# Row maximum of the widest score tile: two parts chained, in place of two parts joined

## The chip, the cores and the metric

The kernel runs on one core of a Trainium2 chip. The metric is the device time of one execution in microseconds (us). Five engines work side by side, each through its own queue of instructions in a fixed order: TensorE (PE, matrix products and transposes into PSUM), VectorE (DVE), ScalarE (ACT), GpSimd (POOL) and SyncE (SP, which here only issues DMAs; ACT issues some too). They meet through semaphores.

## The reference

Causal attention with a decay bias for 4 batches of 8 heads, 576 positions, head size 64, then two feed-forward layers over all 2304 tokens:

```python
scores = scale * np.matmul(q, k.transpose(0, 1, 3, 2))
cum = np.cumsum(np.maximum(s, 0.0), axis=-1)
bias = -(cum[:, :, :, None] - cum[:, :, None, :])
scores = np.where(causal, -1000000000.0, scores + np.minimum(bias, 0.0))
scores = scores - np.max(scores, axis=-1, keepdims=True)
attn = np.exp(scores)
attn = attn / (np.sum(attn, axis=-1, keepdims=True) + 1e-09)
out = np.matmul(attn, v)
...
h = x @ w_in;  e = np.exp(h - h_max);  solu = h * e / (sum(e) + 1e-09)
x = (layer norm of solu, times g_ln) @ w_out
h = x @ w2_in;  out = (h * np.clip(h + 3.0, 0.0, 6.0) / 6.0) @ w2_out
```

The change concerns the row maximum (`np.max`) that is subtracted before `exp`.

## The kernel before, in words

**The scores of a head.** The 576 queries of a head are cut into five tiles of 128, 128, 128, 96 and 96 rows (`SZ`, L197). Because of the causal mask, tile t only needs the keys up to its own end, so its width w is 128, 256, 384, 480 or 576. PE writes the scores into a PSUM bank of 512 columns. The fifth tile, 576 wide, doesn't fit into one bank: `pieces_of` (L518) cuts it into two pieces of 288 columns in two banks, and the other four tiles are one piece each. There are 32 heads, so 32 such wide tiles with 64 pieces.

**The row maximum.** `tops` (L497) runs on DVE once per piece: it adds the mask (0 or -1e30) to the negative scores, writes them to SBUF (`ys`) and collects the smallest value of each row, which is the negative row maximum, into a column of `nmax`. On the chip this is a pair: the pass itself (CUSTOM_DVE_ANT_0) and a short one that reads the accumulator out (DVE_READ_ACCUMULATOR2_ANT). The first piece's minimum goes to column t (here 4), the second's to the spare column NQ (5). `both` in `exps` (L507, its instruction on L508) then takes the smaller of the two columns, and `exp` (L510) runs on ACT over the whole 576 columns with column t as its bias.

**Where the results go.** `norm` (L580) takes the reciprocal of the row sums on DVE and scales the rows on POOL (L587). `tr` transposes them on PE (L614), ACT and DVE copy them to SBUF (L618), `av` multiplies with V on PE (L642). Heads 0 to 7 (batch 0) are done in pairs by `qk_whole` (products on L544), heads 8 to 31 one at a time by `qk` (products on L571). For these, `prep_qk` (L433) loads q and k of a pair (`load_qk`, DMA on L381), transposes them on PE (L450), splits them into a high and a low part on ACT (L458) and DVE (L462), and copies these by DMA into two operand stacks, `stack0` for the even and `stack1` for the odd head (L468, L469, gates L472). A stack is overwritten only when the products of the head that used it are done. The DMAs of q and k of pair p+1 are held until the copies of the keys of pair p into `stack1` have begun (`begun`, L371).

**The first feed-forward layer** runs among the attention of batches 1 to 3: products on L713, statistics (L724 to L754), transposes on L779, products on L800. Its weights arrive as 64-bit words and are decoded by `split64` (L286) on ACT, DVE and POOL during batch 0 and the start of batch 1; their DMAs (raw_wi, raw_wo) are issued by ACT, 512 KB each. The second layer (L957, L988) follows, from about 390 us on.

**The order.** Nothing is issued in the order of the source. Each `plan.add` (L53) records an operation with its engine, an assumed cost, and the keys that it reads and writes. `Plan.emit` (L88) then simulates the engines with these assumed costs, always takes the ready operation with the lowest record number, gives out the eight PSUM banks as they come free, and emits the operations of all engines in the order of the simulated starts. So an operation that is taken out, or a dependency that is added, can move every later operation on every engine. The joining operation is one of these records, at an assumed 0.2 us:

```python
if len(pieces) > 1:
    plan.add("DVE", 0.2, both, reads=[f"nmax{h}_{NQ}"], writes=[f"nmax{h}_{t}"])
```

Of the kernel before, what the change touches and what calls it, by code (L numbers as in the profile page):

```python
# [16 lines left out]
ALU = mybir.AluOpType  # L17
# [144 lines left out]
def dve(n):  # L162
    return 0.15 + 0.00104 * n
# [6 lines left out]
def act(n, extra=0.17):  # L170
    return extra + 0.00085 * n
# [6 lines left out]
def pe(n):  # L178
    return max(0.107, 0.000447 * n)
# [3 lines left out]
def kernel(ctx, tc, q, k, v, s, w_in, w_out, g_ln, w2_in, w2_out, out):  # L183
    nc = tc.nc
# [14 lines left out]
    NQ = len(SZ)  # L199
# [11 lines left out]
    nmax = const.tile([P, NH, NQ + 1], F32, name="nmax")  # L211
# [20 lines left out]
    at = ExitStack()  # L232
# [5 lines left out]
    def bank(key):  # L238
        return banks[plan.bank[key]]


    mask = ap1.tile([P, 480 + P], F32, name="mask")
# [107 lines left out]
    plan = Plan()  # L350
# [17 lines left out]
    raws, vs, ys, x_b, pts, hls = {}, {}, {}, {}, {}, {}  # L368
# [31 lines left out]
    def gates_at(p, j):  # L400
        return stack_t[p % 2][j * D : (j + 1) * D, 2:4, :]
# [91 lines left out]
    def y_key(h, t):  # L493
        p = h // 2
        return f"yz{p}/{h}_{t}" if p < NPAIR and p % 2 else f"y{h}_{t}"

    def tops(h, t, c0, c1, at, key):  # L497

        n, w = SZ[t], ST[t] + SZ[t]
        nc.vector.tensor_tensor_reduce(  # L500
            out=ys[h, t][:n, c0:c1], in0=bank(key)[:n, : c1 - c0], in1=mask[:n, 480 + n - w + c0 : 480 + n - w + c1], scale=-1.0, scalar=3.0e38,
            op0=ALU.add, op1=ALU.min, accum_out=nmax[:n, h, at : at + 1])

    def exps(h, t, pieces):
        n, w = SZ[t], ST[t] + SZ[t]

        def both():  # L507
            nc.vector.tensor_tensor(nmax[:n, h, t : t + 1], nmax[:n, h, t : t + 1], nmax[:n, h, NQ : NQ + 1], ALU.min)  # L508

        def exp():  # L510
            y = ys[h, t]
            nc.scalar.activation(out=y[:n], in_=y[:n], func=AF.Exp, bias=nmax[:n, h, t : t + 1], scale=-1.0, accum_out=sums[:n, h, t : t + 1])  # L512

        if len(pieces) > 1:
            plan.add("DVE", 0.2, both, reads=[f"nmax{h}_{NQ}"], writes=[f"nmax{h}_{t}"])
        plan.add("ACT", act(w, 0.46), exp, reads=[f"nmax{h}_{t}"] + [f"{y_key(h, t)}/{c0}" for c0, _, _ in pieces], writes=[f"{y_key(h, t)}/e", f"sums{h}_{t}"])

    def pieces_of(t):  # L518
        w = ST[t] + SZ[t]
        return [(0, w, t)] if w <= 512 else [(0, w // 2, t), (w // 2, w, NQ)]  # L520

    def qk_whole(p, t):

        n, w = SZ[t], ST[t] + SZ[t]
        heads = (2 * p, 2 * p + 1)
        z_key = f"yz{p}" if p % 2 else None

        def mm(c0, c1, keys):
            if z_key and not (heads[0], 0) in ys:
                for h, tag in zip(heads, ("zh", "zl")):  # L530
                    z = bcp.tile([P, KFF, 2 * P], F32R, tag=tag, name=f"{tag}y{p}", bufs=1).rearrange("p a n -> p (a n)").bitcast(F32)
                    o = 0
                    for i in range(NQ):
                        ys[h, i] = z[:, o : o + ST[i] + SZ[i]]
                        o += ST[i] + SZ[i]
            elif c0 == 0 and not z_key:
                for h in heads:
                    ys[h, t] = ap2.tile([P, w], F32, tag=f"y{t}", name=f"y{h}_{t}")
            for m in range(2):
                for j in range(2):  # L540
                    r = slice(j * D, (j + 1) * D)
                    g, hl = gates_at(p, j), hls[f"HL{p}"].bitcast(F32)[r]
                    a, b = (hl[:, 0, :], hl[:, 1, :]) if m else (g[:, 0, :], g[:, 1, :])
                    nc.tensor.matmul(bank(keys[j])[:n, : c1 - c0], lhsT=a[:, ST[t] : w], rhs=b[:, c0:c1], start=(m == 0), stop=(m == 1))  # L544

        pieces = pieces_of(t)
        for c0, c1, at in pieces:
            keys = [f"sc{h}_{t}_{c0}" for h in heads]
            new = []
            if z_key and z_key not in plan.born:  # L550
                new = [("z", 1, z_key)]
            elif c0 == 0 and not z_key:
                new = [(f"y{t}", 2, f"y{h}_{t}") for h in heads]
            plan.add("PE", 5 * pe(c1 - c0) + 0.1, lambda c0=c0, c1=c1, keys=keys: mm(c0, c1, keys),
                     reads=[f"HL{p}/{x}{c}" for x in "qk" for c in (0, 3)] + [f"G{p}", f"whole{p % 2}"], writes=keys, new=new, bank=keys, after=[f"sc{heads[0]}_{t}_0"] if c0 else [])
            for h, key in zip(heads, keys):
                plan.add("DVE", dve(c1 - c0), lambda h=h, c0=c0, c1=c1, at=at, key=key: tops(h, t, c0, c1, at, key), reads=[key],
                         writes=[f"{y_key(h, t)}/{c0}", f"nmax{h}_{at}"])
        for h in heads:
            exps(h, t, pieces)  # L560

    def qk(h, t):
        n, w = SZ[t], ST[t] + SZ[t]
        pieces = pieces_of(t)

        def mm(c0, c1, key):
            if c0 == 0:
                ys[h, t] = ap2.tile([P, w], F32, tag=f"y{t}", name=y_key(h, t))
            ss = stack_t[h % 2]
            for m in range(2):  # L570
                nc.tensor.matmul(bank(key)[:n, : c1 - c0], lhsT=ss[:, 2 - 2 * m, ST[t] : w], rhs=ss[:, 3 - 2 * m, c0:c1], start=(m == 0), stop=(m == 1))  # L571

        for c0, c1, at in pieces:
            key = f"sc{h}_{t}_{c0}"
            plan.add("PE", 2 * pe(c1 - c0), lambda c0=c0, c1=c1, key=key: mm(c0, c1, key),
                     reads=[f"S{h // 2}_{h % 2}/{x}" for x in "qkg"], writes=[key], new=[(f"y{t}", 2, y_key(h, t))] if c0 == 0 else [], bank=key)
            plan.add("DVE", dve(c1 - c0), lambda c0=c0, c1=c1, at=at, key=key: tops(h, t, c0, c1, at, key), reads=[key], writes=[f"{y_key(h, t)}/{c0}", f"nmax{h}_{at}"])
        exps(h, t, pieces)

    def norm(h):  # L580
# [291 lines left out]
    for b, share in enumerate(SHARES):  # L872
# [10 lines left out]
        while cost < share or in_sum:  # L883
# [3 lines left out]
            c, f, _, in_sum = side.pop(pick)  # L887
# [118 lines left out]
    plan = Plan()  # L1006
# [11 lines left out]
    plan = Plan()  # L1018
# [68 lines left out]
```

## Time and profile before

| | us |
|---|---|
| median of 3 runs | 865.81 (861.31 to 867.98) |
| the profiled execution, its time | 866.15 |
| its span, first to last instruction | 864.3 |
| PE busy in the span | 817.4 (95%) |
| DVE busy | 485.1 (56%) |
| ACT busy | 401.3 (46%) |
| POOL busy | 225.8 (26%) |

The mean granted TensorE clock of the span is 0.986 of full speed. Busy time of PE is the sum over matmul records that overlap a little, so start-to-start distances are the safer measure of its pace. "Idle before" is the time an engine stood still just before an instruction, with the instruction that released it.

### The profile page before, as it was taken

Reading aid. Unit: us, or ns where it says so; the run is one execution under the profiler, and the core shown is the slowest. Engines: PE = TensorE matmul, PEld = TensorE weight load, DVE = VectorE, ACT = ScalarE, POOL = GpSimd, SP = SyncE. Lnnn points to the kernel's source line nnn. Section 1 sums busy time; section 2 is a strip of 40 time slices with the busy share of each in tenths; the row PEclk is TensorE's granted clock in tenths of the full one; section 3 lists DMA queues with packets and bytes.
Section 4 is the critical chain, followed back from the end, with each engine's and each line's share of the span. In section 5 each row is a group of like instructions: output and inputs, shape, how many; then the busy total and the mean of one; then the engine's idle time right before and its main releaser. Section 6 shows DMA issues by size and latency. Waiting matters only on the chain.

```text
span 864.3 us, 13509 instructions
## 1 busy us (share of the span) xinstructions
PE 817.4 (95%) x4816; PEld 690.2 (80%) x4816; DVE 485.1 (56%) x1205; ACT 401.3 (46%) x928; POOL 225.8 (26%) x323
## 2 busy tenths in 40 slices
PE   4987869999999999998989999999999999999998
PEld 3666648888888878886989899998888888888886
DVE  5897897556856576637673999943322232213221
ACT  2875566555755566635353555443221322232222
POOL 2676664524632355234330211200000000000000
PEclk9998979999999999999999999999999999999999
DMA  7468762646645455314313444213000200010001
GB/s 185 122 165 180 165 156 67 144 109 132 126 99 131 114 126 121 86 30 151 103 65 116 147 146 127 94 49 98 0 1 2 76 22 1 1 49 1 1 1 49
DMA packets 93667, 76.85 MB, mean 89 GB/s; under 512 B 62080, under 2 KB 75904, under 8 KB 93600
## 3 DMA queue, kind: packets, MB, share of 16 engines
q1 hardware_dynamic: 91296, 67.60, 31.5%
q10 hardware_dynamic: 2304, 8.39, 3.1%
q8 instruction: 38, 0.62, 0.3%
q14 instruction: 29, 0.24, 0.1%
HBM read 44.71 MB, written 10.03 MB: 63 GB/s over the span
## 4 chain that ended last, share of the span: by engine, by line
PE 78%; DMA 9%; DVE 6%; POOL 3%; SPq 2%; ACT 1%; issue 1%; ACTq 0%; POOLq 0%; DVEq 0%
PE bank L957 22%; PE bank L988 22%; PE bank L800 10%; PE bank L713 7%; PE bank L571 4%; PE bank L614 4%; PE bank L642 4%; DMA rawk<-in_k_dram 2%; DMA rawq<-in_q_dram 2%; PE bank L779 2%; PE bank L450 2%; PE bank L544 1%; POOL y L587 1%; DMA raw_w2o<-in_moe_w_out_dram 1%; DMA raw_w2i<-in_moe_w_in_dram 1%
## 5 line engine op out<-in xcount | busy, mean ns | idle before, releaser
L957 PE MATMUL bank<-x2h,w 128*128 128x512 f32 (+1 forms) x640 | 185.4, 371 | 0.0
L988 PE MATMUL bank<-w,gh 128*128 128x512 f32 x576 | 178.4, 393 | 0.7 <-ACT gh L969 0.7
L965 DVE SCALAR_TENSOR_TENSOR g<-g,bank 128x512 f32<-128x512 f32 (+1 forms) x80 | 50.5, 632 | 184.0 <-ACT g L961 183.8
L957 PEld LDWEIGHTS bank<-x2h,w 128*128 128x128 f32 x640 | 118.6, 188 | 18.7
L961 ACT ACTIVATE g<-bank 128x512 f32<-128x512 f32 (+1 forms) x80 | 44.4, 555 | 176.9 <-PE bank L957 176.7
L988 PEld LDWEIGHTS bank<-w,gh 128*128 128x128 f32 x576 | 107.9, 188 | 23.2 <-ACT gh L969 1.1
L957 PE MATMUL bank<-x2l,w 128*128 128x512 f32 (+1 forms) x320 | 118.5, 370 | 0.0
L988 PE MATMUL bank<-w,gl 128*128 128x512 f32 x288 | 111.5, 391 | 0.0
L587 POOL TENSOR_SCALAR y<-y,rsum 128x128 f32<-128x128 f32 (+4 forms) x140 | 80.6, 592 | 103.0 <-DVE rsum L583 38.2
L512 ACT ACTIVATE y<-y,nmax 128x256 f32<-128x256 f32 (+4 forms) x140 | 83.3, 596 | 41.1 <-DVE nmax L500 30.7
L500 DVE CUSTOM_DVE_ANT_0 y<-bank,mask 96x288 f32<-96x288 f32 (+4 forms) x168 | 73.9, 466 | 49.1 <-PE bank L571 44.2
L800 PE MATMUL bank<-zh,w_out_h 128*128 128x256 f32 x288 | 83.1, 289 | 0.2 <-DVE nmax L500 0.2
L800 PE MATMUL bank<-zl,w_out_h 128*128 128x256 f32 x288 | 81.3, 282 | 2.1 <-DVE zl L786 2.0
L800 PE MATMUL bank<-zh,w_out_l 128*128 128x256 f32 x288 | 81.0, 281 | 0.0
L973 DVE TENSOR_TENSOR gl<-g,gh 128x512 fp32r<-128x512 f32 (+1 forms) x80 | 55.2, 691 | 36.3 <-ACT gh L969 35.6
L969 ACT CAST gh<-g 128x512 fp32r<-128x512 f32 (+1 forms) x80 | 46.1, 578 | 45.2 <-DVE g L965 44.8
L957 PEld LDWEIGHTS bank<-x2l,w 128*128 128x128 f32 x320 | 60.0, 188 | 8.2
L988 PEld LDWEIGHTS bank<-w,gl 128*128 128x128 f32 x288 | 54.1, 188 | 11.9
L713 PE MATMUL bank<-w_in_h,xh 128*128 128x512 f32 x144 | 61.1, 425 | 0.9 <-DVE xh L695 0.9
L571 PE MATMUL bank<-stack 128*96 128x288 f32 (+4 forms) x288 | 59.6, 323 | 0.8 <-issue 0.8
L713 PE MATMUL bank<-w_in_h,xl 128*128 128x512 f32 x144 | 57.6, 400 | 1.3 <-POOL xl L699 1.3
L713 PE MATMUL bank<-w_in_l,xh 128*128 128x512 f32 x144 | 57.4, 399 | 0.0
(166 smaller groups left out, 1394.7 us busy)
## 6 DMA issues: line engine op xcount, KB each, us to landing
raw_w2i<-in_moe_w_in_dram SPq DMA_DIRECT2D x16, 512.0 KB
raw_w2o<-in_moe_w_out_dram SPq DMA_DIRECT2D x16, 512.0 KB
rawq<-in_q_dram SPq DMA_DIRECT2D x32, 144.0 KB
rawk<-in_k_dram SPq DMA_DIRECT2D x32, 144.0 KB
x_d<-x2s SPq DMA_DIRECT2D x36, 128.0 KB
out_dram<-ob SPq DMA_DIRECT2D x18, 256.0 KB
raw_wi<-in_moe_w_in_dram ACTq DMA_DIRECT2D x8, 512.0 KB
raw_wo<-in_moe_w_out_dram ACTq DMA_DIRECT2D x8, 512.0 KB
```

Source lines behind the costliest of these rows:

```text
L500: nc.vector.tensor_tensor_reduce(out=ys[h, t][:n, c0:c1], in0=bank(key)[:n, : c1 - c0], in1=mask[:n, 480 + n - w + c0 : 480 + n - w + c1], ...
L512: nc.scalar.activation(out=y[:n], in_=y[:n], func=AF.Exp, bias=nmax[:n, h, t : t + 1], scale=-1.0, accum_out=sums[:n, h, t : t + 1])
L571: nc.tensor.matmul(bank(key)[:n, : c1 - c0], lhsT=ss[:, 2 - 2 * m, ST[t] : w], rhs=ss[:, 3 - 2 * m, c0:c1], start=(m == 0), stop=(m == 1))
L587: nc.gpsimd.tensor_scalar(ys[h, t][:n], ys[h, t][:n], rsum[:n, h, t : t + 1], 1.0, ALU.mult, ALU.mult)
L713: nc.tensor.matmul(bank(key), lhsT=xs[i][m // 2][:, kk, :], rhs=(w_in_l if m == 1 else w_in_h)[:, kk, f * 512 : (f + 1) * 512], start=(kk ...
L800: nc.tensor.matmul(bank(key)[:, : 2 * P], lhsT=w[:, kk, m * P : (m + 1) * P], rhs=z[:, kk, :], start=(kk == 0 and i == 0), stop=(kk == KFF ...
L957: nc.tensor.matmul(bank(key)[:, :w], lhsT=wt[:, a, 0, c * P : (c + 1) * P], rhs=x[:, c, :w], start=(c == 0 and i == 0), stop=(c == KDM - 1 ...
L961: nc.scalar.activation(out=g_t[ci, m][0][:, :w], in_=bank(key)[:, :w], func=AF.Relu, bias=3.0, scale=1.0)
L965: nc.vector.scalar_tensor_tensor(out=gg, in0=gg, scalar=6.0, in1=bank(key)[:, :w], op0=ALU.min, op1=ALU.mult)
L969: nc.scalar.copy(gh[:, :w], gg[:, :w])
L973: nc.vector.tensor_sub(gl[:, :w], gg[:, :w], gh[:, :w].bitcast(F32))
L988: nc.tensor.matmul(bank(key), lhsT=g_t[ci, m][1 + i // 2][:, t * P : (t + 1) * P], rhs=w2[m][:, i % 2, 1, :], start=(m == 0 and i == 0), s ...
```

## The change

The first piece now leaves its minimum in the spare column NQ, the second piece starts its minimum from that column (the scalar operand of the pass is a column of `nmax` in place of the constant 3.0e38) and writes the final value to column t. The joining instruction and its record are gone; the second piece's record reads the spare column.

```diff
     def tops(h, t, c0, c1, at, key):
         n, w = SZ[t], ST[t] + SZ[t]
+        above = nmax[:n, h, NQ : NQ + 1] if c0 else 3.0e38
         nc.vector.tensor_tensor_reduce(
-            out=ys[h, t][:n, c0:c1], in0=bank(key)[:n, : c1 - c0], in1=mask[...], scale=-1.0, scalar=3.0e38,
+            out=ys[h, t][:n, c0:c1], in0=bank(key)[:n, : c1 - c0], in1=mask[...], scale=-1.0, scalar=above,
             op0=ALU.add, op1=ALU.min, accum_out=nmax[:n, h, at : at + 1])
...
-        def both():
-            nc.vector.tensor_tensor(nmax[:n, h, t : t + 1], nmax[:n, h, t : t + 1], nmax[:n, h, NQ : NQ + 1], ALU.min)
-        if len(pieces) > 1:
-            plan.add("DVE", 0.2, both, reads=[f"nmax{h}_{NQ}"], writes=[f"nmax{h}_{t}"])
...
     def pieces_of(t):
-        return [(0, w, t)] if w <= 512 else [(0, w // 2, t), (w // 2, w, NQ)]
+        return [(0, w, t)] if w <= 512 else [(0, w // 2, NQ), (w // 2, w, t)]
...
-            plan.add("DVE", dve(c1 - c0), ..., reads=[key], writes=[f"{y_key(h, t)}/{c0}", f"nmax{h}_{at}"])
+            plan.add("DVE", dve(c1 - c0), ..., reads=[key] + [f"nmax{h}_{NQ}"] * (c0 > 0), writes=[f"{y_key(h, t)}/{c0}", f"nmax{h}_{at}"])
```

Since the planner lays out its order anew, instructions move on all engines. Lines after L499 carry numbers up to four lower or one higher in the changed file (L500 becomes L501, L571 L567, L713 L709, L779 L775). Three places:

**DVE, the wide tiles of heads 0 and 1, at about 24 us.** y_4 is the 576-wide tile, one buffer per head. Before:

```order
L500 ISA y_4_246,nmax<-bank_96,mask 96x288
L500 ISA nmax 96x1
L500 ISA y_4_247,nmax<-bank_97,mask 96x288
L500 ISA nmax 96x1
L500 ISA y_4_246,nmax<-bank_98,mask 96x288
L500 ISA nmax 96x1
L500 ISA y_4_247,nmax<-bank_99,mask 96x288
L500 ISA nmax 96x1
L508 TENSOR_TENSOR nmax<-nmax 96x1 x2
```

and now:

```order
L501 ISA y_4_246,nmax<-bank_96,mask 96x288
L501 ISA nmax 96x1
L501 ISA y_4_247,nmax<-bank_97,mask 96x288
L501 ISA nmax 96x1
L501 ISA y_4_246,nmax<-bank_98,mask,nmax 96x288
L501 ISA nmax 96x1
L501 ISA y_4_247,nmax<-bank_99,mask,nmax 96x288
L501 ISA nmax 96x1
```

The two joining instructions are gone and the second pieces read `nmax`. This happens for all 32 heads; for 20 of them the second piece now stands directly behind the first one's pair.

**PE, between the products of head 12 and the transposes of q and k of pair 7, at about 115 to 129 us.** L571 are products of head 12 (stack_109 is its stack), L779 transposes of the first layer's first token tile, L450 the transposes of the loaded q, L713 products of its third token tile. Before:

```order
L571 MATMUL bank_97<-stack_109 128x384 x2
L571 MATMUL bank_100<-stack_109 128x128 x2
L571 MATMUL bank_98<-stack_109 96x288 x2
L571 MATMUL bank_101<-stack_109 96x288 x2
L571 MATMUL bank_103<-stack_109 128x256 x2
L571 MATMUL bank_96<-stack_109 96x480 x2
L779 MATMUL bank_97<-ident,e_995 128x128 x4
L779 MATMUL bank_99<-ident,e_995 128x128 x4
L450 MATMUL bank_102<-ident,rawq_1331 128x96 x3
L571 MATMUL bank_97<-stack_110 96x288 x2
L450 MATMUL bank_100<-ident,rawq_1331 128x96 x3
L713 MATMUL bank_98<-w_in_h,xh_1345 128x512
```

and now (the rows left out are nine more of L709):

```order
L567 MATMUL bank_96<-stack_109 128x384 x2
L567 MATMUL bank_98<-stack_109 128x128 x2
L567 MATMUL bank_102<-stack_109 96x288 x2
L567 MATMUL bank_100<-stack_109 96x288 x2
L775 MATMUL bank_103<-ident,e_1031 128x128 x4
L775 MATMUL bank_97<-ident,e_1031 128x128 x4
L709 MATMUL bank_103<-w_in_h,xh_1176 128x512
L709 MATMUL bank_103<-w_in_l,xh_1176 128x512
L709 MATMUL bank_103<-w_in_h,xl_1177 128x512
...
L450 MATMUL bank_96<-ident,rawq_1313 128x96 x3
L450 MATMUL bank_101<-ident,rawq_1313 128x96 x3
```

Twelve products of the first layer now stand ahead of the q transposes, and four products of head 12 (128x256, 96x480) behind them.

**SP, the copies of pair 5 into the stacks, at about 73 to 86 us.** HL5q and HL5k are the split q and k of pair 5 (heads 10 and 11), stack_109 is stack0, stack_110 stack1. Before:

```order
L468 DMA stack_109<-HL5q 64x576
L469 DMA stack_109<-HL5q 64x2x576
L468 DMA stack_109<-HL5k 64x576
L469 DMA stack_109<-HL5k 64x2x576
L472 DMA stack_109<-rows_d 4x2x576
L468 DMA stack_110<-HL5q 64x576
L469 DMA stack_110<-HL5q 64x2x576
L468 DMA stack_110<-HL5k 64x576
```

and now:

```order
L468 DMA stack_109<-HL5q 64x576
L469 DMA stack_109<-HL5q 64x2x576
L468 DMA stack_110<-HL5q 64x576
L469 DMA stack_110<-HL5q 64x2x576
L468 DMA stack_109<-HL5k 64x576
L469 DMA stack_109<-HL5k 64x2x576
L472 DMA stack_109<-rows_d 4x2x576
L468 DMA stack_110<-HL5k 64x576
```

The copy of q into stack1, which has to wait for head 9, now stands ahead of the copies of k into stack0, which head 10 needs.

## Rows read from the trace of the kernel before

**Rows 1.** Busy time by stretch: columns PE, PEld, DVE, ACT, POOL, clock, DMA share, GB/s

```profile
0.00:140.00 140.00, 106.48 (x710) 80.79 (x712) 109.29 (x326) 85.03 (x225) 80.23 (x108) 0.91 0.68 160
140.00:380.00 240.00, 237.86 (x1782) 206.50 (x1779) 149.94 (x496) 143.52 (x384) 98.50 (x165) 1.00 0.49 109
```

**Rows 2.** What PE waited for: us in total, times, longest

```profile
PE bank L450 <- DMA rawq<-in_q_dram: 10.9, 4, 5.0
PE bank L450 <- DMA rawk<-in_k_dram: 3.0, 3, 2.2
PE bank L779 <- DVE nmax L500: 2.2, 1, 2.2
```

**Rows 3.** Groups of DVE instructions by form: count, busy us, mean ns, idle before

```profile
L500 DVE CUSTOM_DVE_ANT_0 y<-bank,mask 96x288 f32<-96x288 f32 x56 | 23.5, 447 | 10.3 <-PE bank L571 9.8
L335 DVE TENSOR_TENSOR w<-a_w2i,w 128x512 fp32r<-128x512 f32 x16 | 11.0, 686 | 0.3 <-ACT w L329 0.2
L508 DVE TENSOR_TENSOR nmax<-nmax 96x1 f32<-96x1 f32 x32 | 9.1, 291 | 0.7
L583 DVE RECIPROCAL rsum<-rsum 128x5 f32<-128x5 f32 x32 | 6.1, 190 | 1.1
L333 DVE SCALAR_TENSOR_TENSOR w_out_l<-a_wo,g_sb,w_out_h 128x512 fp32r<-128x512 f32 x8 | 6.1, 757 | 1.6 <-ACT w_out_h L325 1.6
L738 DVE TENSOR_SCALAR st<-st 128x1 f32<-128x1 f32 x18 | 3.8, 214 | 0.6
```

**Rows 4.** Busy time by stretch of 20 us, columns as in rows 1

```profile
100.00:120.00 20.00, 17.71 (x105) 13.24 (x106) 19.72 (x51) 13.53 (x34) 10.31 (x13) 1.00 0.52 142
120.00:140.00 20.00, 13.84 (x69) 11.03 (x69) 14.57 (x36) 11.57 (x29) 10.03 (x13) 0.66 0.71 158
```

**Rows 5.** Chain that ended last, 95 to 130 us: start, us, what

```profile
101.10 1.08 DVE nmax L508
...
116.31 7.29 DMA raw_wo<-in_moe_w_out_dram
```

**Rows 6.** Timeline of POOL and of DVE at 101 us: start, us, instruction

```profile
100.88 1.29 POOL L321 TENSOR_TENSOR a_wo<-a_wo,e_wo 128x512 f32<-128x512 f32 x1 [4.61 <-DVE e_wo L317]
...
101.02 1.17 DVE L508 TENSOR_TENSOR nmax<-nmax 96x1 f32<-96x1 f32 x1
```

**Rows 7.** Timeline of PE, 87 to 134 us: start, us, instruction, idle before

```profile
87.34 0.39 PE L713 MATMUL bank<-w_in_h,xh 128*128 128x512 f32 x1
...
89.20 0.39 PE L713 MATMUL bank<-w_in_h,xl 128*128 128x512 f32 x1
...
115.09 2.49 PE L571 MATMUL bank<-stack 128*128 128x384 f32 x12
...
121.85 1.12 PE L779 MATMUL bank<-ident,e 128*128 128x128 f32 x4 [1.14 <-DVE st L734]
127.98 0.71 PE L450 MATMUL bank<-ident,rawq 96*128 96x96 f32 x3 [5.01 <-DMA rawq<-in_q_dram]
...
132.60 0.63 PE L713 MATMUL bank<-w_in_h,xh 128*128 128x512 f32 x1
133.03 0.63 PE L713 MATMUL bank<-w_in_l,xh 128*128 128x512 f32 x1
```

**Rows 8.** Timeline of SP's DMA issues, 76 to 86 us: start, us

```profile
76.68 0.50 SPq L472 DMA_DIRECT2D stack<-rows_d  x1
81.59 0.46 SPq L468 DMA_DIRECT2D stack<-HL5q  x1
...
83.42 1.67 SPq L469 DMA_DIRECT2D stack<-HL5k  x1
```

**Rows 9.** Chain that ended last, at 59 us: one stack copy

```profile
59.32 6.96 DMA stack<-HL4q
```

**Rows 10.** Timeline of PE between heads 9 and 10

```profile
82.34 0.48 PE L571 MATMUL bank<-stack 128*96 128x288 f32 x2
...
92.11 0.44 PE L450 MATMUL bank<-ident,rawq 96*128 96x96 f32 x3 [2.10 <-DMA rawq<-in_q_dram]
```

More of the change, by code (lines that the diff above doesn't have):

```diff
@@ L499, in tops @@
         n, w = SZ[t], ST[t] + SZ[t]
+        above = nmax[:n, h, NQ : NQ + 1] if c0 else 3.0e38
         nc.vector.tensor_tensor_reduce(
-            out=ys[h, t][:n, c0:c1], in0=bank(key)[:n, : c1 - c0], in1=mask[:n, 480 + n - w + c0 : 480 + n - w + c1], scale=-1.0, scalar=3.0e38,
+            out=ys[h, t][:n, c0:c1], in0=bank(key)[:n, : c1 - c0], in1=mask[:n, 480 + n - w + c0 : 480 + n - w + c1], scale=-1.0, scalar=above,
             op0=ALU.add, op1=ALU.min, accum_out=nmax[:n, h, at : at + 1])
@@ L556, in qk_whole @@
             for h, key in zip(heads, keys):
-                plan.add("DVE", dve(c1 - c0), lambda h=h, c0=c0, c1=c1, at=at, key=key: tops(h, t, c0, c1, at, key), reads=[key],
+                plan.add("DVE", dve(c1 - c0), lambda h=h, c0=c0, c1=c1, at=at, key=key: tops(h, t, c0, c1, at, key), reads=[key] + [f"nmax{h}_{NQ}"] * (c0 > 0),
                          writes=[f"{y_key(h, t)}/{c0}", f"nmax{h}_{at}"])
@@ L576, in qk @@
                      reads=[f"S{h // 2}_{h % 2}/{x}" for x in "qkg"], writes=[key], new=[(f"y{t}", 2, y_key(h, t))] if c0 == 0 else [], bank=key)
-            plan.add("DVE", dve(c1 - c0), lambda c0=c0, c1=c1, at=at, key=key: tops(h, t, c0, c1, at, key), reads=[key], writes=[f"{y_key(h, t)}/{c0}", f"nmax{h}_{at}"])
+            plan.add("DVE", dve(c1 - c0), lambda c0=c0, c1=c1, at=at, key=key: tops(h, t, c0, c1, at, key), reads=[key] + [f"nmax{h}_{NQ}"] * (c0 > 0), writes=[f"{y_key(h, t)}/{c0}", f"nmax{h}_{at}"])
         exps(h, t, pieces)
```

## Prediction

> **What bounds the kernel now.** I read the busy time by stretch first [rows 1]. From 140 us on PE is busy 237.9 of 240 us until 380 us, at full clock (1.00, which is the 2.4 GHz level), and the change neither adds nor removes a PE instruction. DVE is busy 149.9 of these 240 us. So after 140 us a shorter DVE queue shows only where PE waits for it, and PE has 2.1 us of idle time to give. Before 140 us it is different: PE is busy 106.5 of 140 us, so 33.5 us are idle, and the mean granted clock is 0.91. DVE is busy 109.3 us there. That is where the change can act, and there are two ways: DVE work that sits on the path, and the order, which the planner lays out anew.
>
> Next, what PE waits for [rows 2]. The largest entries that the change can reach are the transposes of q and k (L450), which wait 10.9 us in four holes for q and 3.0 us for k, and one hole of 2.2 us in front of L779, put down to a pass of the row maximum on DVE. These holes end with a DMA, not with DVE. But the DMAs start when earlier work frees their queue, and how long PE stands still depends on how much other work the order puts in front of the waiting transposes.
>
> **The change part by part.**
>
> *The joining instruction.* There are 32 of them, 9.1 us together, 291 ns on average [rows 3]. That is an upper bound, because the mean is raised by a few long ones. At 101.02 us one took 1.17 us for one element per row. POOL had begun a two-operand pass at 100.88 us that lasted 1.29 us, so both ended at 102.2 us [rows 6]. The joining operation reads two SBUF operands, and it was held until POOL was done. What is saved by its removal goes by place. Thirteen stand before 140 us by the order (two for each of the four pairs of batch 0, and heads 8 to 12), nineteen behind it, where PE is the bound; those I cost at nothing, covered by the PE work of rows 1. Of the thirteen, the one at 101 us lies on the chain that ended last, with 1.08 us [rows 5], in a stretch where DVE is busy 19.72 of 20 us [rows 4]. The chain leads from there over DVE to a weight transfer that begins at 116.31 us [rows 5] and is followed by the q transfer that ends PE's longest hole. I take 1.1 us for it. The other twelve at 291 ns are 3.5 us of DVE time that I leave out of the sum and keep as a bound, since DVE waits for PE or DMA between them.
>
> The Trainium skill, "SBUF — State Buffer", section "Who interferes with whom", says that a VectorE instruction with two SBUF inputs contends with a GpSimd instruction that reads SBUF, and one with at most one SBUF input does not. The 1.17 us of rows 6 agree. The page doesn't say whether a per-row scalar operand counts as an input; if it does, the new second pieces, which read the mask and a column of `nmax`, would fall under it, which is the fourth rival below.
>
> *The chained pass.* The 32 second pieces read a column as scalar operand, and wait for it on DVE's own semaphore. The pass itself costs 447 ns [rows 3] and the trace shows it only with a constant. From both sides: a pass with such an operand and two SBUF tensors (L333) takes 757 ns against 686 ns for a two-operand one without it (L335), at the same 512 columns, so at most 71 ns more; a one-column operation with two such operands (L738) takes 214 ns, so the operand by itself is no visible price, and I bound it from below by zero, as nothing in it could make the pass shorter [rows 3]. Over 32 that is 0 to 2.3 us of DVE, of which the thirteen early ones are 0 to 0.9 us. The wait is no new one: the joining operation also waited for the accumulator read just before it, and a dependent short operation with such a wait (L583) shows 1.1 us of idle time over 32 instances [rows 3], 34 ns each. I take zero for both. Behind a held second piece stands the rest of DVE's queue, and for it wait ACT's exponential and then POOL and PE; the exponential itself now comes one DVE instruction earlier.
>
> *The new order.* At 128 us PE stood still for 5.01 us before the q transposes of pair 7 [rows 7]. Before, it did twelve products of head 12 (2.49 us from 115.09 us), eight transposes L779 until 122.97 us, and then waited. Now twelve products of the first layer stand ahead of these transposes, and four of the twelve products of head 12 behind them. The nine matmuls that start from 87.34 to 89.20 us are 0.2325 us apart, so twelve are 2.79 us of cover that comes in. The four that go out have 2 x 256 + 2 x 480 = 1472 of 3648 columns, an estimated 1.0 us of the 2.49 us. So 1.8 us of the hole is filled, if the first layer's third tile is ready. The order speaks for that: its cast stood behind the e passes of the tile before it on DVE and now stands ahead of them. I take 1.8 us.
>
> *SP.* Moves that I cost at nothing: the copy of q into stack1 now stands ahead of the copies of k into stack0. Before, SP issued all three parts of stack0 by 77.2 us and then stood until 81.59 us for head 9 [rows 8]; now the keys of head 10 have to wait for that too. The first issue after that wait came at 81.59 us, and with the two copies of q into stack1 ahead of them the copies of k leave by about 83.4 us, where the fourth issue stood before [rows 8]. A stack copy took 6.96 us [rows 9], so they land at about 90.4 us. PE finished head 9 at 82.8 us and, in the old order, had work until 92.11 - 2.10 = 90.0 us [rows 10]; in the new one about as much (transposes and V products) stands ahead of head 10. So it is just covered. The loads of k of pair 6 pass two V loads, which would bring them forward; nothing is counted for that.
>
> Sum, against the profiled execution's own 866.15 us: 866.15 - 1.1 - 1.8 = 863.3 us. The median of the runs is 865.81 us, 0.3 us below that execution, so the forecast is 2.5 us under the median. Its own range: lower by the slow clock behind the 5 us hole (the granted clock is 0.66 in 120 to 140 us [rows 4]; L713 starts are 0.43 us apart at 133 us against 0.2325 us at full clock [rows 7], and nine matmuls at that pace lose 1.8 us) and by the twelve other early joinings at 3.5 us less what DVE would wait anyway, say 2.7 us: 858.8 us. Higher by 2.3 us for the scalar operand and by the 1.8 us if the hole stays as long: 867.4 us.
>
> **The rivals.**
>
> *The holes only move.* All work in the first 140 us hangs on the same transfers; what PE does earlier it can't do later. For it: the holes end with DMAs [rows 2]. Against it: a hole at 2.4 GHz filled by ready work is time gained, as PE is the bound behind. Only the joining at 101 us counts: 866.15 - 1.1 = 865.1 us.
>
> *The new order closes several holes.* Half of the 16.1 us of rows 2 goes (8.0 us), the clock stays up behind the longest (1.8 us), with the 1.1 us: 866.15 - 8.0 - 1.8 - 1.1 = 855.3 us. For it: the pair 6 transposes also get six products of head 10 in front. Against it: these displace twelve L713, and the hole for pair 5 keeps its place in the order.
>
> *The keys of head 10 come late.* It decides if the copies of k into stack0 queue behind a weight transfer. These are 512 KB and take 7.29 us [rows 5]. The copies would land at 83.42 + 7.29 + 6.96 = 97.7 us and PE, out of work at 90.0 us, would stand 7.7 us, and lose 1.8 us more to the low clock behind such a hole: 863.3 + 7.7 + 1.8 = 872.8 us, slower than before. For it: the order on SP. Against it: weight transfers are issued by ACT at its own pace, and none has to fall there. Below a hole of about 2.9 us it is no loss.
>
> *The scalar operand is held by POOL* as the joining operation was, now in a long pass. If each of the thirteen early ones is held as long as the joining of rows 6 took, 13 x 1.17 = 15.2 us come on DVE in front of everything: 863.3 + 15.2 = 878.5 us. Against it: L738 has two such operands and a mean of 214 ns [rows 3].
>
> **How the numbers follow.** I give the forecast 0.45, the holes that only move 0.15, several closed holes 0.19, the late keys 0.13, the held operand 0.08. A measurement of this kernel can tell about 1% from no change: below 857.2 us or above 874.5 us. Faster comes from the closed holes (0.14 of their 0.19) and a tail of the forecast (0.03): 0.17. Slower comes from the held operand (0.07) and late keys that cost more than worked out (0.05): 0.12. The rest, 0.71, is no change that can be told. The range reaches from 854.5 us (some of the closed holes left out) to 873.0 us (the late keys within, the held operand out).
>
> **What would show it.** DVE would have 32 fewer instructions and about 9 us less in the group of L508, and the second pieces' mean would stay within 71 ns of 447 ns. The wait for q in front of L450 at pair 7 would be about 3 us in place of 5.01 us, and the clock of its stretch above 0.66. From 140 us to 380 us PE would be as busy as before. Wrong would be: second pieces of over 0.6 us; head 10's first products waiting for a stack copy for over 3 us; or a gain that sits behind 140 us.

## The result, and the profile after

The changed kernel takes 870.05 us (median of 14 runs, 868.58 to 875.70), the kernel before 865.67 us beside it on the same chip (14 runs, 861.31 to 867.98). The ratio is 1.0063 with a 95% interval of 1.0047 to 1.0079: slower by 0.6%, where 0.3% faster was forecast. The time lies within the given range, the sign is the other one. The profiled execution took 869.28 us, its span is 867.5 us.

Busy time by stretch, the changed kernel (columns as in rows 1):

```profile
0.00:140.00 140.00, 108.29 (x720) 81.50 (x720) 107.42 (x313) 84.93 (x228) 77.69 (x108) 0.93 0.65 156
140.00:380.00 240.00, 237.25 (x1765) 205.60 (x1766) 147.68 (x475) 143.72 (x382) 99.27 (x164) 0.99 0.50 111
120.00:140.00 20.00, 15.48 (x78) 11.52 (x76) 14.67 (x41) 12.84 (x34) 9.56 (x13) 0.83 0.72 163
140.00:160.00 20.00, 19.19 (x124) 16.11 (x125) 17.17 (x51) 11.84 (x28) 13.73 (x19) 0.91 0.40 93
```

Before 140 us PE is busy 1.8 us more than in rows 1, the size that the forecast wanted, and the clock from 120 to 140 us rose from 0.66 [rows 4] to 0.83. Yet the stretch behind, 140 to 160 us, has a clock of 0.91: something slows PE there (in rows 1 it is 1.00 behind 140 us).

The groups of the row maximum on DVE (count, busy us, mean ns), answering to rows 3:

```profile
L501 DVE CUSTOM_DVE_ANT_0 y<-bank,mask,nmax 96x288 f32<-96x288 f32 x28 | 14.2, 511 | 8.4 <-PE bank L567 5.7 <-DVE nmax L501 0.2 <-PE bank L610 0.2
L501 DVE CUSTOM_DVE_ANT_0 y<-bank,mask 96x288 f32<-96x288 f32 x28 | 12.4, 448 | 5.5 <-PE bank L567 5.2
```

The second pieces are told by the operand `nmax`: 511 ns against 448 ns for the first pieces, so the column as scalar costs 63 ns each, 2.0 us over 32. The group of the joining operation (9.1 us) is gone.

What PE waited for (us in total, times, longest), answering to rows 2:

```profile
PE bank L450 <- DMA rawq<-in_q_dram: 6.2, 3, 3.9
PE bank L450 <- DMA rawk<-in_k_dram: 4.0, 2, 2.4
PE bank L638 <- DVE pt L614: 1.8, 2, 1.6
```

The waits for q fell from 10.9 to 6.2 us, but the longest now stands at pair 6, and a wait of 1.6 us for a copy of the transposed weights (`pt`) is new. In PE's timeline (start, us, instruction, idle time before):

```profile
87.86 1.05 PE L567 MATMUL bank<-stack 128*128 128x384 f32 x6 [0.65 <-DMA stack<-HL5k]
92.82 1.19 PE L450 MATMUL bank<-ident,rawq 96*128 96x96 f32 x6 [3.91 <-DMA rawq<-in_q_dram]
...
121.48 0.79 PE L709 MATMUL bank<-w_in_h,xh 128*128 128x512 f32 x1 [1.23 <-DVE zl L782]
122.07 0.63 PE L709 MATMUL bank<-w_in_l,xh 128*128 128x512 f32 x1
122.49 0.63 PE L709 MATMUL bank<-w_in_h,xl 128*128 128x512 f32 x1
...
126.76 0.97 PE L450 MATMUL bank<-ident,rawq 96*128 96x96 f32 x6
129.27 0.69 PE L450 MATMUL bank<-ident,rawk 96*128 96x96 f32 x6 [1.54 <-DMA rawk<-in_k_dram]
...
137.57 0.58 PE L610 MATMUL bank<-ident,y 96*128 96x96 f32 x4 [0.73 <-DVE pt L614]
138.09 0.44 PE L638 MATMUL bank<-pt,V 128*64 128x128 f32 x4
138.75 0.45 PE L610 MATMUL bank<-ident,y 96*96 96x96 f32 x3 [0.23 <-ACT pt L614]
140.81 4.01 PE L638 MATMUL bank<-pt,V 128*64 128x320 f32 x20 [1.60 <-DVE pt L614]
```

Three places answer to the prediction. At pair 7 (126.76 us) the wait for q is gone: the twelve products of the first layer stand ahead of it. They start 0.43 us apart, the pace of the low clock in rows 7. (That they filled the hole, as forecast, is not yet shown by this: PE may also have come late.) At pair 6 (92.82 us) the wait has grown from 2.10 [rows 10] to 3.91 us: it ends 0.7 us later, and PE, which had twelve products of the first layer in front of it before and has none now, comes to it 1.1 us sooner. And behind pair 7 there are three waits of 0.73, 0.23 and 1.60 us in a row, each for the copy of a group of head 11's transposes, with four products of 0.44 us as the only other work between them; the twenty products behind the last take 4.01 us.

### The profile page after: what moved, and what is told of

Read it like the earlier page. It is cut to its first block, busy times and chain, and to the rows that moved or that the text cites. A ratio compares the mean times of both kernels' runs of the same rounds, so it can differ in the third digit from the quotient of the medians.

```text
span 867.5 us, 13486 instructions
## 1 busy us (share of the span) xinstructions
PE 820.9 (95%) x4816; PEld 692.1 (80%) x4816; DVE 481.4 (55%) x1173; ACT 401.8 (46%) x928; POOL 223.7 (26%) x323
## 4 chain that ended last, share of the span: by engine, by line
PE 82%; DMA 7%; DVE 6%; POOL 2%; SPq 2%; issue 1%; ACT 1%; DVEq 0%; POOLq 0%; ACTq 0%
PE bank L953 23%; PE bank L984 22%; PE bank L796 11%; PE bank L709 9%; PE bank L638 5%; PE bank L567 4%; PE bank L610 4%; DMA rawk<-in_k_dram 2%; PE bank L450 2%; DMA raw_wi<-in_moe_w_in_dram 2%; PE bank L775 1%; DMA rawq<-in_q_dram 1%; POOL y L583 1%; DVE y L501 1%; PE bank L540 1%
## 5 line engine op out<-in xcount | busy, mean ns | idle before, releaser
L510 ACT ACTIVATE y<-y,nmax 128x128 f32<-128x128 f32 (+4 forms) x140 | 83.5, 598 | 39.6 <-DVE nmax L501 38.2
L501 DVE CUSTOM_DVE_ANT_0 y<-bank,mask 128x128 f32<-128x128 f32 (+4 forms) x140 | 62.9, 470 | 48.3 <-PE bank L567 42.4
L796 PE MATMUL bank<-zl,w_out_h 128*128 128x256 f32 x288 | 81.9, 284 | 2.2 <-DVE zl L782 2.2
L796 PE MATMUL bank<-zh,w_out_h 128*128 128x256 f32 x288 | 83.9, 291 | 0.0
L796 PE MATMUL bank<-zh,w_out_l 128*128 128x256 f32 x288 | 81.8, 284 | 0.0
L969 DVE TENSOR_TENSOR gl<-g,gh 128x512 fp32r<-128x512 f32 (+1 forms) x80 | 53.2, 666 | 36.2 <-ACT gh L965 35.6
L709 PE MATMUL bank<-w_in_h,xh 128*128 128x512 f32 x144 | 61.4, 426 | 2.1 <-DVE zl L782 1.2
L567 PE MATMUL bank<-stack 128*96 128x288 f32 (+4 forms) x288 | 58.7, 320 | 2.0 <-DMA stack<-rows_d 1.3
L709 PE MATMUL bank<-w_in_h,xl 128*128 128x512 f32 x144 | 58.1, 403 | 1.0 <-POOL xl L695 1.0
L709 PE MATMUL bank<-w_in_l,xh 128*128 128x512 f32 x144 | 57.9, 402 | 0.0
```

Source lines behind the costliest of these rows:

```text
L501: nc.vector.tensor_tensor_reduce(out=ys[h, t][:n, c0:c1], in0=bank(key)[:n, : c1 - c0], in1=mask[:n, 480 + n - w + c0 : 480 + n - w + c1], ...
L709: nc.tensor.matmul(bank(key), lhsT=xs[i][m // 2][:, kk, :], rhs=(w_in_l if m == 1 else w_in_h)[:, kk, f * 512 : (f + 1) * 512], start=(kk ...
L796: nc.tensor.matmul(bank(key)[:, : 2 * P], lhsT=w[:, kk, m * P : (m + 1) * P], rhs=z[:, kk, :], start=(kk == 0 and i == 0), stop=(kk == KFF ...
L969: nc.vector.tensor_sub(gl[:, :w], gg[:, :w], gh[:, :w].bitcast(F32))
```

## The experiments

Each ratio is against the kernel before on the same chip, with its 95% interval. The experiments came in four sets on three chips, in which the kernel before took 862.39 to 865.63 us, so most differences of two ratios below cross chips. One profile is one execution, and it tells less than a ratio: three kernels whose order is the old one up to 100 us (chain_old_order, new_last, middle_b) ended pair 6's transposes at 93.6, 96.8 and 97.6 us in their profiles. So the ratios decide, and a profile shows where.

### Pass or order?

Theory: the new order loses, the chained pass does not. The first kernel chains the passes but leaves the planner a record of the joining operation that emits nothing, so every engine's order is that of before.

```diff
+        if w > 512:
+            at = t if c0 else NQ
+        above = nmax[:n, h, NQ : NQ + 1] if c0 else 3.0e38
...
-            nc.vector.tensor_tensor(nmax[:n, h, t : t + 1], nmax[:n, h, t : t + 1], nmax[:n, h, NQ : NQ + 1], ALU.min)
+            pass
```

> The chained passes of the changed kernel in exactly the order of the kernel before: the planner still gets the joining record, but it emits nothing. If the order makes the loss (theory O): 863 to 866 us, no slower than the kernel before (865.7 us). If the chained pass itself makes it (theory P, its mean is 511 ns in the changed kernel against 447 ns): 869 to 871 us, as the changed kernel (870.05 us).

The second has the old passes, with the joining operation emitted in the same record as the second pass, so that the planner sees what it sees in the changed kernel.

```diff
             op0=ALU.add, op1=ALU.min, accum_out=nmax[:n, h, at : at + 1])
+        if c0:
+            nc.vector.tensor_tensor(nmax[:n, h, t : t + 1], nmax[:n, h, t : t + 1], nmax[:n, h, NQ : NQ + 1], ALU.min)
```

> The old, unchained passes and a joining operation right behind the second piece, in exactly the order of the changed kernel. Theory O: 870 to 873 us, as slow as the changed kernel or slower by what the 32 joinings cost. Theory P: 865 to 867 us, as the kernel before.

The third keeps the old order and passes and leaves out the joining operation (`both` is `pass`; the second part writes column t).

> Leaves out the joining of the two parts (the exponential uses the minimum of the second part alone), in exactly the order of the kernel before: what the 32 joinings cost in place. Theory O: 862 to 866 us, a gain of at most 3 us. Theory P says nothing of this run; were it 4 us or more below the kernel before, the chain would have had much to give and lost it.

The fourth is the kernel before with the planner's cost of the joining operation at 0.1 in place of 0.2: the same instructions, laid out anew.

> The kernel before with one number of the planner changed: the joining operation is assumed to cost 0.1 us in place of 0.2 us. The same instructions in another order (330 of 3506 PE rows move). If a new layout by itself moves the time by some us whatever it is for (theory L): at least 2 us away from 865.7 us, likelier slower than faster. Theory P, and an order that matters only at the places of the changed kernel: within 1.5 us of 865.7 us.

Measured: chain_old_order 860.25 us, 0.9972 (0.9953 to 0.9991). join_new_order 870.03 us, 1.0084 (1.0061 to 1.0107). nojoin_old_order 860.02 us, 0.9971 (0.9955 to 0.9987). before_join01 861.97 us, 0.9995 (0.9979 to 1.0010).

So the edit of the passes alone is a gain of 0.28%, the same as leaving the joining out altogether: of the 63 ns of each second pass (2.0 us in all, 0.23%) the time shows nothing, though the intervals are about as wide. The order alone costs about 0.9% (0.9972 to 1.0063 with chained passes), and it costs it with the old passes too. That any new order would lose is ruled out by before_join01, whose order is new and whose time is that of before.

### Which part of the order?

The planner now makes both lists, with and without the joining record, and the kernel takes a stretch from either. After 947 entries both lists have emitted the same set.

```diff
+TURNS = [("new", 562), ("old", None)]
...
-        for _, i in sorted(order):
+        lists = {"old": self.plan_of(False), "new": self.plan_of(True)}
+        seq = []
+        for which, upto in TURNS:
...
+            seq += [i for i in part if i not in done and (i not in self.joins or not any(w == "new" for w, _ in TURNS))]
+        for i in seq:
             self.ops[i][2]()
```

> Chained passes; the first 562 plan entries (up to head 10's scores, about 100 us) in the changed kernel's order, all that follows in the old order. chain_old_order (old order throughout) was at 0.9972 of the kernel before. Theory 'two places' (the new order loses at pair 6's hole near 90 us, about 2.5 us there, and again near 140 us, about 4 us): this kernel pays the first alone, +2.5 us, ratio about 1.000, with a wait of 3 to 4.5 us for rawq at pair 6. Rival 'one place' (all of the 8 to 10 us come from the stretch near 140 us): ratio 0.997 as the old order. Rival 'spread' (every moved row costs alike; 90 of 381 moved PE rows are here): +2 us, ratio 0.9995, but without a lone long wait.

With `[("old", 562), ("new", 947), ("old", None)]`:

> Chained passes; entries 563 to 947 (about 100 to 158 us) in the changed kernel's order, the rest in the old. Theory 'two places': +4 us over chain_old_order, ratio about 1.002, with waits for copies of pt near 137 to 141 us. Rival 'spread': 232 of 381 moved PE rows, +5 us, ratio 1.003, no place that stands out. Rival 'joint' (the stretch loses only because the first part arrives late): ratio 0.997, and no waits for pt copies.

With `[("old", 947), ("new", None)]`:

> Chained passes; the first 947 entries (to about 158 us) in the old order, all that follows in the changed kernel's order. Theory 'two places': nothing is lost here, ratio 0.997 as chain_old_order. Rival 'spread': +1.5 to 2 us, ratio 0.999. Rival 'tail' (the order after 158 us carries a good part of the loss, since the last 350 us of the two profiles differ by 2 us too): 1.001 or more.

Measured: new_first 869.12 us, 1.0040 (1.0022 to 1.0058). new_middle 867.36 us, 1.0024 (1.0004 to 1.0044). new_last 861.84 us, 0.9945 (0.9927 to 0.9963).

Against 0.9972 the first part costs 0.68%, the middle 0.52%, and the last gains 0.27% (its interval overlaps that of chain_old_order, so the gain isn't certain). That fits "two places", with the first dearer than the 2.5 us expected of it; "spread" doesn't fit, since the first part has 90 moved PE rows and the middle 232. new_last is faster than both kernels of this case.

A splice of two orders has a price of its own, though. At entry 562 three operations that one list has emitted are still missing from the other, and as many the other way (at entry 720, used below, it is eight). Behind that place PE waits twice in new_first where it waits neither in chain_old_order nor in the changed kernel:

```profile
113.70 0.30 PE L662 MATMUL bank<-ident,y 96*128 96x96 f32 x1 [0.74 <-POOL y L635]
115.42 0.80 PE L761 MATMUL bank<-w_in_h,xh 128*128 128x512 f32 x1 [1.42 <-DVE nmax L547]
```

These 2.2 us, 0.25% of the time, belong to the splice and not to the changed kernel's order, so the first part itself may well cost less than 0.68%.

### The place on SP's queue

In the changed kernel SP's issues read (start, us):

```profile
80.60 0.47 SPq L468 DMA_DIRECT2D stack<-HL5q  x1
81.12 0.62 SPq L469 DMA_DIRECT2D stack<-HL5q  x1
81.83 0.56 SPq L468 DMA_DIRECT2D stack<-HL5k  x1
82.48 1.01 SPq L469 DMA_DIRECT2D stack<-HL5k  x1
83.53 0.50 SPq L472 DMA_DIRECT2D stack<-rows_d  x1
...
86.86 1.51 SPq L381 DMA_DIRECT2D rawq<-in_q_dram  x2
```

The copy of q into stack1 waits until 80.60 us, and the three issues for stack0 (81.83 to 84.03 us), which could have gone before, come out behind it. The loads of pair 6 stand last. The first experiment moves only that one entry (391) behind the stack0 entries (402, 403); the order of the other engines stays that of the changed kernel.

```diff
 TURNS = [("new", None)]
+MOVES = [(391, 403)]
...
+        for i, j in MOVES if self.joins else ():
+            seq.remove(i)
+            seq.insert(seq.index(j) + 1, i)
```

> The changed kernel with one entry moved on SP's queue: the copies of HL5q into stack1 stand behind those of HL5k (and the gate rows) into stack0, as in the kernel before; no other engine's order differs. Theory 'SP place': the loads of pair 6's q and k leave some 3 us earlier, the wait for rawq at pair 6 falls from 3.9 us to 1 or 2, and the kernel gains 2 to 3 us: ratio 1.0063 becomes about 1.0035. Rival: the hole only moves (head 10's products or rawk come late instead): ratio stays at 1.006.

Measured: 866.66 us, 1.0011 (0.9995 to 1.0028). Of the 1.0063 of the changed kernel 0.52% goes, more than expected. (Within one set, after_both_mended against after_dve_mended below, the same move gives back 0.62%.) SP and PE in its profile:

```profile
76.47 0.47 SPq L516 DMA_DIRECT2D stack<-HL5k  x1
77.04 0.62 SPq L517 DMA_DIRECT2D stack<-HL5k  x1
77.70 0.67 SPq L520 DMA_DIRECT2D stack<-rows_d  x1
81.40 0.46 SPq L516 DMA_DIRECT2D stack<-HL5q  x1
...
85.05 2.00 SPq L429 DMA_DIRECT2D rawq<-in_q_dram  x2
```

```profile
90.16 0.69 PE L498 MATMUL bank<-ident,rawq 96*128 96x96 f32 x6 [1.42 <-DMA rawq<-in_q_dram]
```

The three issues for stack0 leave at 76.47 us, ahead of the wait; the load of q leaves 1.8 us earlier (85.05 in place of 86.86), and PE's wait at pair 6 falls from 3.91 to 1.42 us. This was a gain in spite of longer waits at pair 7. PE there has the changed kernel's order, with the twelve products of the first layer ahead of these transposes, and still stands for 1.87 us for q and 2.33 us for k; below them chain_old_order, without the twelve:

```profile
121.96 0.69 PE L498 MATMUL bank<-ident,rawq 96*128 96x96 f32 x6 [1.87 <-DMA rawq<-in_q_dram]
124.98 1.19 PE L498 MATMUL bank<-ident,rawk 96*128 96x96 f32 x6 [2.33 <-DMA rawk<-in_k_dram]
```

```profile
123.33 0.71 PE L450 MATMUL bank<-ident,rawq 96*128 96x96 f32 x3 [3.46 <-DMA rawq<-in_q_dram]
```

So with PE no longer held at pair 6, the hole at pair 7 is back: 4.20 us in two pieces (4.12 in after_both_mended) against 3.46 us (3.41 in new_last and 3.51 in old_sp_late below, which have the old order there too).

The converse puts the bad SP order into the good kernel. A first attempt moved the copy of q forward in the program (`[(391, 390)]` on the old order):

> The converse of after_sp_mended: chained passes in the old order (chain_old_order, 0.9972), with the one difference that SP issues the copies of HL5q into stack1 ahead of those of HL5k into stack0, as in the changed kernel. Theory 'SP place': SP waits there for stack1 (until about 80.5 us), head 10's products wait for HL5k, the loads of pair 6 leave some 3 us later, +3 to +4.5 us, ratio 1.001 to 1.0025. Rival (the place hurts only together with the rest of the new order): 0.9972.

Measured: 866.82 us, 1.0043 (1.0020 to 1.0065). In this kernel head 9's last score products come behind the copy in the program and read pair 5's q in place of pair 4's, so SP's wait there isn't that of the changed kernel; nothing is concluded from it. The second attempt moves the copies of k into stack0 back instead (`[(402, 391), (403, 402)]`), and changes no value:

> The converse of after_sp_mended, with every value as in the kernel before: chained passes in the old order (0.9972), and only SP issues the copies of HL5k and the gate rows into stack0 behind the copies of HL5q into stack1, which wait for stack1. Theory 'SP place': head 10's products wait for HL5k and the loads of pair 6 leave up to 3 us later; +3 to +4.5 us, ratio 1.001 to 1.0025. Rival (the place costs only together with the rest of the new order): 0.997 to 0.998.

Measured: 868.93 us, 1.0059 (1.0035 to 1.0084), against 0.9972 a loss of 0.87%, twice the expected and as much as the whole new order costs. PE in its profile, and below in chain_old_order's, whose PE order is the same:

```profile
89.06 0.77 PE L623 MATMUL bank<-stack 128*96 128x288 f32 x2 [7.53 <-DMA stack<-rows_d]
89.76 4.86 PE L694 MATMUL bank<-pt,V 128*64 128x128 f32 x24
```

```profile
82.66 0.48 PE L574 MATMUL bank<-stack 128*96 128x288 f32 x2 [1.41 <-DMA stack<-HL5k]
83.07 2.55 PE L645 MATMUL bank<-pt,V 128*64 128x128 f32 x24
```

In the old PE order head 10's first product stands early, so the late copies stop PE itself for 7.53 us, and the 24 products behind the hole take 4.86 us instead of 2.55; at pair 6 it then doesn't wait at all. So the place costs in either order, but by another path: in the changed kernel by the loads of pair 6, as after_sp_mended's profile has it, here by head 10's keys themselves. Three DMA issues, in front of two others or behind them, are worth 0.5 to 0.9% here.

### The place on VectorE behind pair 7

DVE ahead of the wait at 140.81 us, in the changed kernel:

```profile
137.84 0.42 DVE L309 TENSOR_SCALAR a_wo<-a_wo 128x512 int32<-128x512 int32 x1
138.29 1.38 DVE L314 TENSOR_SCALAR e_wo<-a_wo 128x512 int32<-128x512 int32 x1
139.70 0.69 DVE L317 SCALAR_TENSOR_TENSOR e_wo<-raw_wo,e_wo 128x512 f32<-128x512 uint32 x1
140.31 0.45 DVE L614 COPY pt<-bank 96x288 f32<-96x288 f32 x1
```

The copy that PE waits for stands behind three steps that decode w_out. The experiment puts the copy ahead of them (`MOVES = [(503, 759), (520, 503), (523, 520)]` on the changed kernel's order).

> The changed kernel with one place on VectorE mended: the last copy of head 11's transposed weights (96x288, it ends the wait of 1.60 us at 140.81 us) stands ahead of the three decode steps of w_out's part 5 instead of behind them; nothing else moves. Theory 'two places': the wait of 1.60 us falls to about 0.5, the kernel gains 1 to 1.5 us, ratio 1.0063 becomes about 1.0047. Rival: the products behind it wait for something else that is as late (decoded w_out, zl): ratio unchanged.

With SP's place mended as well:

> The changed kernel with both mended places, SP's and VectorE's. after_sp_mended alone was at 1.0011. If the gains add: about 0.9995 to 1.000. If the SP place alone does it: 1.001.

Measured: after_dve_mended 870.39 us, 1.0078 (1.0052 to 1.0103); after_both_mended 864.99 us, 1.0016 (0.9994 to 1.0037). The place itself did as expected, in after_dve_mended's profile:

```profile
144.39 2.33 PE L694 MATMUL bank<-pt,V 128*64 128x320 f32 x20 [0.61 <-DVE pt L670]
```

The wait is 0.61 us in place of 1.60, and the same twenty products take 2.33 us in place of 4.01. The kernel's time shows nothing of it: 1.0078 and 1.0063 overlap, 1.0016 and 1.0011 too. In that profile a wait of 1.13 us for POOL has come in at 155.59 us. A gain of 1 us (0.12%) would be lost in these intervals; one of 0.5% would not. So this copy's place on DVE is not where the middle part loses its 0.5%, and the expected 1.0047 did not come.

### The middle part, and whether the parts add

Of the middle part, the second half alone (`[("old", 720), ("new", 947), ("old", None)]`):

> Chained passes; old order for the first 720 entries (through pair 7's transposes and head 11's first), the changed kernel's order for entries 721 to 947, the old behind. new_middle (563 to 947) was at 1.0024, the old order at 0.9972. Theory 'late decode' (the loss of the middle lies behind pair 7: head 11's transposes with no products between them, w_out's parts decoded later): 1.001 to 1.0025. Rival 'pair 7' (the loss lies before entry 720, in the way to pair 7's waits): 0.997 to 0.998.

And the new order at both ends, SP's place mended, the old order between (`[("new", 562), ("old", 947), ("new", None)]` and `MOVES = [(391, 403)]`):

> Chained passes; the changed kernel's order up to entry 562 with SP's place mended, the old order from 563 to 947, the changed kernel's behind. If the four measured parts add (0.9972, first +0.0068, SP's place -0.0052, last -0.0027): 0.996. If the gain of SP's place depends on the changed middle: 0.999 to 1.001.

Measured: middle_b 867.34 us, 1.0029 (1.0006 to 1.0052), as much as new_middle: the loss of the middle lies behind entry 720, that is behind pair 7's transposes. ends_new_sp_mended 865.08 us, 1.0017 (0.9996 to 1.0037), where the sum of the parts was 0.996: the parts don't add, but five intervals of about 0.2% stand in that sum, and taken together (0.44%) they leave little of the gap of 0.56%. Its profile has a wait of 4.08 us for q at pair 7 (3.46 in chain_old_order), and the two waits of 0.74 and 1.42 us behind the splice that new_first has.

Two things tell the new middle from the old in the traces. One is the place of head 11's transposes. In chain_old_order its last eleven stand in one piece behind the products, and no wait follows:

```profile
133.32 1.16 PE L617 MATMUL bank<-ident,y 96*128 96x96 f32 x11
134.32 0.60 PE L782 MATMUL bank<-ident,e 128*128 128x128 f32 x4
134.85 2.98 PE L645 MATMUL bank<-pt,V 128*64 128x256 f32 x28
```

In the changed kernel they come in three pieces (136.29, 137.57 and 138.75 us) with the waits shown above. The other is when the next work that could fill such holes is there. The first layer's first product with w_out (L800, L803, L796) starts, in the kernel before, in chain_old_order and in the changed kernel (middle_b's, 151.27 us, is as late):

```profile
143.45 0.33 PE L800 MATMUL bank<-zh,w_out_h 128*128 128x256 f32 x1
```

```profile
138.78 0.33 PE L803 MATMUL bank<-zh,w_out_h 128*128 128x256 f32 x1
```

```profile
151.75 0.28 PE L796 MATMUL bank<-zh,w_out_h 128*128 128x256 f32 x1
```

In the old order these products come 8 us behind the end of pair 7's transposes (130.9 us in chain_old_order), in the changed kernel 22 us behind (130.0 us). The twelve products with w_in that the new order put ahead of pair 7 can no longer fill these holes, the next 24 stand behind them (from 144.75 us on), and those with w_out come later still. That is read from the traces; no run put other work back there, so it stays an argument.

## Why the prediction was wrong

*The joining operation (-1.1 us): right in sign.* chain_old_order is 2.1 us under the kernel before (862.39 to 860.25 us); its interval, 0.8 to 4.1 us, has the 1.1 us in it. The twelve other early joinings, which the prediction kept as a bound of 2.7 us, took 2.0 us together in the trace of the kernel before.

*The chained pass (zero): right.* The price of the operand is 63 ns, inside the bound of 71 ns, and chain_old_order (0.9972) is level with the kernel without any joining (0.9971). The rival in which POOL holds the operand fell. Ten of the 32 second pieces began while POOL was in a two-operand pass; they took 501 to 515 ns, and none of the 32 over 515. DVE first, then POOL, in the changed kernel:

```profile
81.24 0.52 DVE L501 CUSTOM_DVE_ANT_0 y<-bank,mask,nmax 96x288 f32<-96x288 f32 x1
```

```profile
80.20 1.29 POOL L335 TENSOR_TENSOR w_in_l<-a_wi,w_in_h 128x512 fp32r<-128x512 f32 x1 [2.23 <-ACT w_in_h L329]
```

The Trainium skill, "DVE: scalar operands, raw-bit mode, write accounting and state across instructions", section "1. Scalar operands", says that a per-partition scalar does not take up the second tensor stream; these rows agree, and so the rule of "SBUF — State Buffer" that the prediction weighed does not reach it.

*The new order (-1.8 us): the step that failed.* "So 1.8 us of the hole is filled" seems to have happened: the hole of 5.01 us at pair 7 became one of 1.54 us for k. But PE comes to it only at 126.76 us, late from pair 6 and behind twelve products at the pace of the low clock; in chain_old_order the hole was over at 123.33 us. In after_sp_mended PE comes in time, with the same twelve products in front, and stands 4.20 us, against 3.46 us in chain_old_order. So as far as these profiles show, one of each kernel, the twelve products bought nothing: the hole moved. And the step looked only at the hole where work came in, and not at the places that this work left: the part of the order behind pair 7's transposes alone costs 0.5% (middle_b, new_middle), for which the sum has no term.

*SP (nothing): the second step that failed.* "So it is just covered" came true for the one consumer that was looked at: head 10's products waited 0.65 us for their keys, which left at 81.83 and 82.48 us against a forecast of "by about 83.4 us". That was luck in part. The row at 82.34 us [rows 10], read as the end of head 9, is head 10's first product; in chain_old_order the same instruction waits 1.41 us for the keys (HL5k). And the keys were there at 87.86 us, not at 90.4, while PE was out of work at 87.2 us, not at 90.0: two errors that cancel. The loss came by what was not priced: the issues that moved behind the wait also pushed back what stood behind them on the queue, the loads of pair 6 (86.86 us, 85.05 with the place mended), where PE then waited 3.91 us. Mending the place gives back 0.52%. The sentence on those loads counted two V loads that they pass, and not the copies that now pass them.

*The rivals.* The late keys of head 10 (872.8 us) came nearest to the measured 870.05 us and named the right queue, but with another mechanism: no copy queued behind a weight transfer. "The holes only move" (865.1 us) describes what pair 7 shows, a hole that is back when PE comes in time and others opened behind it, but it had no loss in it. "A gain that sits behind 140 us" did not come; the changed kernel's PE is busy 0.6 us less there from 140 to 380 us, and slower in clock.

What stays open: why the middle part costs 0.5%, beyond the two readings above, with one of its waits for copies mended and the time unchanged; and how much of the first part's loss and of the gap in the sum is the splice.

## What to carry to other kernels

Where a planner lays out the order, removing a cheap instruction is two edits: the instruction, and a new order for everything behind it. Keep the old order by leaving the planner a record that emits nothing, time both, and take the better: here the pass gains 0.28% and its new order loses 0.9%. When work comes in to fill a hole, look for the place it left, and if the hole is gone, ask whether the engine merely came late to it; when a DMA issue moves behind a wait on an in-order queue, price every issue behind it, not only the consumer of the one that moved.

## What the runs showed of the hardware

A column as scalar operand of the masked minimum costs 63 ns on a pass of 288 columns (511 against 448 ns; in nojoin_old_order, with the constant in both pieces, none took over 456 ns), and POOL held none of the ten such passes that began inside one of its own. A one-operand integer pass on DVE was held: L314 took 1.38 us at 138.29 us while POOL ran the row below, and 0.43 us at 129.12 us with POOL idle. Two more such steps took 1.06 us (L309, 112.74 us) and 1.33 us (L314, 145.26 us), each begun inside a POOL pass of 1.3 us.

```profile
138.07 1.31 POOL L695 TENSOR_TENSOR xl<-x,xh 128x512 fp32r<-128x512 f32 x1 [3.86 <-PE bank L610]
```

```profile
129.12 0.43 DVE L314 TENSOR_SCALAR e_wo<-a_wo 128x512 int32<-128x512 int32 x1
```

The Trainium skill, "SBUF — State Buffer", section "Who interferes with whom", lists such scalar passes among those that can enter a mode with two ports and then contend with GpSimd; these rows agree. Its exemption of passes with at most one SBUF input holds only outside those modes, a condition that the prediction's sentence on it left out.

A hole can cost more than its length, by the granted clock behind it. The same 24 products take 2.55 us behind a wait of 1.41 us (clock 1.00, chain_old_order) and 4.86 us behind one of 7.53 us (0.51, old_sp_late: almost all at the 1.2 GHz level); twenty others take 2.33 us behind 0.61 us (1.00, after_dve_mended) and 4.01 us behind 1.60 us, the third wait within 4 us (0.57, the changed kernel). Not every hole does it: behind the 1.56 us before 90.57 us in chain_old_order the clock stayed at 1.00.
